# An RWKV-7 and mixture kernel: TensorE's order written out in passes 1 to 4, x placed one piece later, raw transfers and stores moved on SyncE's queue

## The chip, the cores and the metric

The kernel runs on one core of a Trainium2 chip. The metric is the device time of one execution in microseconds (us), lower is better. Engines are called as in the profile: PE is TensorE's matmuls, PEld its weight loads, DVE is VectorE, ACT is ScalarE, POOL is GpSimd, and SP is SyncE, which here only issues transfers.

## The reference

Two blocks follow each other. The first is a recurrence over 768 tokens for 4 batches and 8 heads of width 40, the second a mixture of four experts over the 3072 rows that come out of it.

```python
for t in range(S):                      # S = 768, state is (4, 8, 40, 40)
    y[:, :, t] = einsum('bhd,bhde->bhe', rt, state)
    Sa = einsum('bhde,bhe->bhd', state, at)
    state = state * wt[:, :, None, :] - einsum('bhd,bhe->bhde', Sa, bt) + einsum('bhd,bhe->bhde', vt, kt)
x = y.transpose(0, 2, 1, 3).reshape(3072, 320)
p = domain_probs / (domain_probs.sum(-1, keepdims=True) + 1e-09)
for e in range(4):                      # w1[e] is 320 x 1024, w2[e] is 1024 x 320
    out += p[:, e:e+1] * (np.maximum(x @ w1[e], 0) @ w2[e])
```

All numbers are float32.

## The kernel before

The 768 tokens are cut into 12 chunks of 64. A *unit* is one chunk of two batches, so there are 24 units; units 2c and 2c+1 make chunk c.

What a unit needs without the state is in the generator `within`, cut into steps by `yield`. For units 3 and later: (W1) `G`, the running product of the decays, from `rawW` by a transpose on DVE; (W2) `pg` on PE, `gp` and its reciprocal on DVE (L418, L419); (W3) `N` and `K` (L455, L459), `AT` (L228, L463) and the transposes of `rawV` and `rawR` into `VT` and `RT` (L228), all on DVE; (W4) `pNT` and `pKT` on PE (L340) with copies on ACT (L441); (W5) `pc` from `VT` and `RT` (L376) and the masked copy into `VC` on DVE (L387); (W6) `pfe` (L376) and the copy of `F` on ACT (L489); (W7) the masked copy `ET` on DVE (L387); (W8) `pev` on PE.

`substitute` solves a triangular system for all heads of a unit: a few instructions on DVE (`blocks`, `M`, L528 to L550) and then a chain of small operations on `Z`, on GpSimd for units 2 and later (L555 to L572). `merge` turns the result (`Qc`, `QTc`, L583 and L585), copies it with GpSimd (`QT`, L591), and joins it on PE by `pY` and `pQ` (L599), with copies of `Yq` on ACT between the two (L606).

What needs the state is in `step`: (S1) `prn`, `RH` on DVE; (S2) `psat`, `SaT` on ACT; (S3) `pxr`, the masked copy `SX` on DVE; (S4) `pdy`, `Y` and the new state on DVE (L694 to L705); (S5) x, the transposed input of the mixture: for the first two chunks by 12 matmuls into `pxT` (L711) and a copy (L715), later by 12 transfers on SyncE (L723).

The mixture is cut into *pieces* that wait in the list `todo`. For units 0 and 1 it is done unit by unit (`mixture_of_unit`): an *up* (w1 with Relu, `ph` and `hs`, L738, L752, L757) comes in pairs, a *down* (w2, `po`, L796) follows, and its product is added to `osb` on DVE (L771, L773); the last down of a unit also stores its rows (L778). From chunk 1 on a piece works on both units of a chunk (`mixture_of_chunk`): wide ups, sums of `hs` on DVE (`a`, L867), and products `down_1` and `down_2` (L873). Weights come in `w1p` or `sums` (L287), each load begun when the piece that used its buffer is done.

Pass u of the main loop runs the rest of W for unit u+1, S3 to S5 of unit u, W of unit u+2, the substitution of unit u+2, the merge of unit u+1 and S1, S2 of unit u+1. At four places, `gap(0)` to `gap(3)`, it takes pieces from `todo`. Passes 1 to 4 are *early* (`EARLY = 5`, so `u < EARLY`; pass 0 stands ahead of the loop); they take one piece a gap, and two at gaps 2 and 3 of pass 4.

The order in which instructions stand in the program is not the order in which they run. A scheduler simulates the program and gives each engine, at each moment, the earliest instruction that is ready in its simulation; the orders that come out are fixed for the run. `keep_in_program_order` ties an instruction behind the one that was written before it on the same engine; it adds no wait. In the kernel before, the early units' instructions on DVE, the substitution and the weight loads are tied so; of the matmuls only a few are.

`load_raw` makes transfers of the raw inputs; those of V and R of unit u+3, 16 of them, go into the list `later`, from which `begin_later` takes six after each piece (three where a gap takes two), and, in every pass, what is left, ahead of the second piece:

```python
        begin_later(len(later))
        run(w, 1)
        if not early:
            run(m, 1)
        gap(1)
```

Of the kernel before, what the change touches and what calls it, by code (L numbers as in the profile page):

```python
# [15 lines left out]
def kernel(  # L16
# [38 lines left out]
    nc = tc.nc  # L55
# [3 lines left out]
    P = 128  # L59
# [4 lines left out]
    NF = F // P  # L64
    NU = NC * B // 2
    DT = DM - 2 * P

    const = ctx.enter_context(tc.tile_pool(name="const", bufs=1))
    sb = ctx.enter_context(tc.tile_pool(name="sb", bufs=1))
# [98 lines left out]
    EARLY = 5  # L168
# [137 lines left out]
    def normalize():  # L306
        n = B // 2 * NC
        pp = big("pp")
        flat = probs.rearrange("p i t e -> p (i t) e")
        for e in range(E):  # L310
            nc.tensor.transpose(out=pp[:, e * n:(e + 1) * n], in_=flat[:, :, e], identity=ident[0:n, 0:n])
# [24 lines left out]
    def turn(name, src, pinned=False):  # L336

        p = big(name)
        for j in range(NJ):
            ins = nc.tensor.transpose(out=p[:, j * P:(j + 1) * P], in_=src(j), identity=ident[:])  # L340
            if pinned and j == 0:
                tc.keep_in_program_order(ins)
        return p
# [26 lines left out]
    def quadrants(p, lo, order, out_cols, *terms):  # L370


        for j, s, i in order:
            for n, term in enumerate(terms):
                row, col, at, lhsT, rhs = term(j, s, i)
                nc.tensor.matmul(  # L376
                    out=p[row][half(col), lo + at * out_cols:lo + (at + 1) * out_cols], lhsT=lhsT, rhs=rhs,
                    start=(n == 0), stop=(n == len(terms) - 1),
                )
        return [by(x[:, lo:lo + NJ * out_cols], out_cols) for x in p]  # L380
# [197 lines left out]
    def merge(q):  # L578


        Qc = sb.tile([P, H, Q], FP32, name="Qc", tag="q", bufs=2)
        QTc = sb.tile([P, H, Q], FP32, name="QTc", tag="q", bufs=2)
        tc.keep_in_program_order(nc.vector.transpose(out=dealt(Qc[:]), in_=q.Z))  # L583
        tc.keep_in_program_order(
            nc.vector.transpose(  # L585
                out=QTc[:].rearrange("p h r -> p (h r)"), in_=Qc[:].rearrange("p h c -> p (h c)"),
            )
        )
        q.QT = QTs()
        for i in range(P // Q):  # L590
            ins = nc.gpsimd.tensor_copy(out=q.QT[quarter(i), :, quarter(i % 2)], in_=QTc[quarter(i)])  # L591
            tc.keep_in_program_order(ins)
        yield

        def two_heads(name, lhsT, rhs, to):
            p = big(name)
            for n in range(NJ):
                for r in range(2):
                    nc.tensor.matmul(  # L599
                        out=p[half(r), n * 2 * Q:(n + 1) * 2 * Q], lhsT=lhsT[half(r), 2 * n:2 * n + 2, :],  # L600
                        rhs=rhs[half(r), 2 * n:2 * n + 2, :], start=True, stop=True,
                    )
# [12 lines left out]
    def step(q, xT):  # L615
# [92 lines left out]
        if placed:  # L708
            px = big("pxT")
            for n, (g, j) in enumerate(PLACES):  # L710
                nc.tensor.matmul(  # L711
                    out=px[:, g * P:(g + 1) * P], lhsT=pick[:, n, :], rhs=Y[:, j].rearrange("p i t -> p (i t)"),
                    start=(n == 0 or PLACES[n - 1][0] != g), stop=(n + 1 == len(PLACES) or PLACES[n + 1][0] != g),
                )
            nc.scalar.copy(out=xT, in_=px[:, 0:3 * P].rearrange("p (g t) -> p g t", g=3))  # L715
# [14 lines left out]
    def up_last(k, xT, n):  # L730

        w1 = pieces[k]
        ph = [ps.tile([P, HF // 2, n], FP32, name="ph", tag="mm", bufs=3) for _ in range(2)]

        for f in range(HF // 2):
            for c in range(2):
                for i in range(2):
                    nc.tensor.matmul(  # L738
                        out=ph[i][half(c), f, :], lhsT=w1.last[part(i), f, half(c)],
                        rhs=xT[part(i), 2, :], start=(f == 0), stop=False,  # L740
                    )
        return ph

    def up_main(k, xT, n, ph):

        w1 = pieces[k]
        h = sb.tile([P, HF, 2 * P], FP32, name="hs", tag="hs", bufs=3)
        for i in range(2):
            for f in range(HF // 2):
                for g in range(2):  # L750
                    at = i * HF // 2 + f
                    nc.tensor.matmul(  # L752
                        out=ph[i][:, f, :], lhsT=w1.main[:, g, at * P:(at + 1) * P],
                        rhs=xT[:, g, :], start=False, stop=(g == 1 and f == HF // 2 - 1),
                    )
# [27 lines left out]
    def mixture_of_unit(q):  # L783

        hs, at = {}, 2 * E * q.u

        def ups(e):
            hs[e] = [up(at + 2 * e + x, q.xT, P) for x in range(2)]
            used(at + 2 * e + 2)
            if q.u == 0 and e + 2 < E:  # L790
                load_w2(e + 2)

        def down(e):
            po = ps.tile([P, DM], FP32, name="po", tag="mm", bufs=3)
            for f in range(NF):
                nc.tensor.matmul(  # L796
                    out=po[:], lhsT=hs[e][f // HF][:, f % HF, 0:P], rhs=w2_sb[e][:, f, :],
                    start=(f == 0), stop=(f == NF - 1),
                )
            if e == 0:  # L800
                q.osb = outputs()
            add(q.osb[:], po[:], scale(q, e), e == 0)
            if e == E - 1:
                store(q, q.osb)

        todo.append(lambda: ups(0))
        for e in range(E):
            todo.append(lambda e=e: down(e))
            if e + 1 < E:
                todo.append(lambda e=e: ups(e + 1))  # L810
# [25 lines left out]
    def mixture_of_chunk(qs, xT):  # L836
# [32 lines left out]
        def products(name, *terms):  # L869
            p = ps.tile([P, len(terms) * HD], FP32, name=name, tag="mm", bufs=3)  # L870
            for n, (a, b) in enumerate(terms):
                for f in range(HF):
                    nc.tensor.matmul(  # L873
                        out=p[:, n * HD:(n + 1) * HD], lhsT=a[:, f, :], rhs=b[:, f, :],
                        start=(f == 0), stop=(f == HF - 1),
                    )
            return p
# [52 lines left out]
        last[:] = before  # L930


    todo, last, later = [], [], []

    def begin_later(n):
        for move in later[:n]:
# [3 lines left out]
    def mix(n):  # L940

        for piece in todo[:n]:
            piece()
            begin_later(3 if n > 1 else 6)
        del todo[:n]

# [22 lines left out]
    def keep_warm(n):  # L969

        for _ in range(n):
            ins = nc.tensor.matmul(out=warm[:, 0:P], lhsT=ident[:], rhs=ident[:], start=True, stop=True)
            tc.keep_in_program_order(ins)

    ws = [within(units[u]) for u in range(3)]
# [79 lines left out]
    sums_at.update({4 * 4 + 3: 2, 4 * 5 + 0: 3, 4 * 5 + 1: 2, 4 * 5 + 2: 3})  # L1055
    sum_ops = (None for e in range(E) for _ in add_weights(e))
    for u in range(1, NU):
        q = units[u]
        m = s_next = w = w_next = iter(())
        if u + 1 < NU:  # L1060
# [8 lines left out]
            mix((1 if at in sparse else 2) if pieces is None else pieces)  # L1069

        early = u < EARLY
        run(w_next, 99 if early else 1)
        run(s, 1)
        gap(0)
# [16 lines left out]
        gap(1)  # L1091

        if u + 3 < NU:
            go(load_raw(begin(u + 3), "WA"))
# [39 lines left out]
        s = s_next  # L1134
# [31 lines left out]
```

## Time and profile before

| | before |
|---|---|
| three timed runs | 1135.22, 1136.07, 1136.14 us (median 1136.07) |
| profiled execution | 1129.6 us, span of the instructions 1127.5 us |
| mean granted clock of TensorE | 0.986 |
| TensorE idle from 94.1 to 243.9 us (passes 1 to 4) | 14.2 of 149.8 us |
| TensorE idle from 287 to 1127 us | 9.8 of 840 us |

The span is that of one profiled execution. A stretch's idle time is its length less the busy time of TensorE in it, from the busy times by stretches. The names of tiles in the profile have no unit numbers: units are told apart by the order of their appearance. Names are written out<-in, and a line such as L376 or L752 is that of the helper that records the matmul, so blocks are told apart by the tile they write. A transfer's row on SyncE is the time of its issue, not of the data.

### The profile page before, as it was taken

The page shows a single profiled execution, that of the slowest core. Times are in us where ns is not written, and L with a number is a line of the kernel's source. Part 1 is how long each engine was busy: PE and PEld are TensorE (multiplying, and loading weights), DVE is VectorE, ACT ScalarE, POOL GpSimd, SP SyncE. Part 2 cuts the span into 40 slices and gives each one's busy share as a digit, 9 for nine tenths or more (in the row PEclk, how much of TensorE's full clock was granted, in tenths as well). Part 3 has the DMA queues.
Part 4 walks back from the last instruction along what each step waited for, and adds up shares of the span by engine and source line. Part 5 has one row for each costly group of instructions (what it writes and reads, how often), then busy time and mean ns, then how long its engine had stood idle before and what let it go on. Part 6 is the DMA issues. An engine that isn't in the chain of part 4 may idle for free.

```text
span 1127.5 us, 38551 instructions
## 1 busy us (share of the span) xinstructions
PE 1083.1 (96%) x16100; PEld 963.2 (85%) x16100; DVE 758.8 (67%) x1553; ACT 353.0 (31%) x956; POOL 498.8 (44%) x1272
## 2 busy tenths in 40 slices
PE   6899997999999999999999999999999999999998
PEld 5777776788989889988989989989899999888887
DVE  8766547797766767677677677677677686553343
ACT  2323423332332332432432332332333323321110
POOL 5005727754625526437437347346346356340000
PEclk7899998999999999999999999999999999999999
DMA  7784553245253543644543543544553442231320
GB/s 118 214 239 125 130 113 71 71 108 126 77 130 88 122 102 99 141 103 93 143 104 88 143 103 90 142 96 96 133 114 86 122 110 63 76 90 57 108 90 12
DMA packets 268868, 122.18 MB, mean 108 GB/s; under 512 B 213736, under 2 KB 242072, under 8 KB 268696
## 3 DMA queue, kind: packets, MB, share of 16 engines
q1 hardware_dynamic: 265416, 119.12, 43.4%
q8 instruction: 127, 2.08, 0.8%
q10 hardware_dynamic: 3280, 0.61, 0.3%
q14 instruction: 45, 0.37, 0.1%
HBM read 111.79 MB, written 3.93 MB: 103 GB/s over the span
## 4 chain that ended last, share of the span: by engine, by line
PE 67%; POOL 10%; DVE 7%; issue 4%; ACT 2%; SPq 1%; DMA 1%; DVEq 0%; POOLq 0%
PE p L873 23%; PE ph L752 22%; PE ph L738 7%; POOL Z L572 6%; POOL Z L559 4%; PE pdy L376 2%; PE psat L376 2%; PE po L796 2%; DVE M L534 1%; PE pxr L376 1%; PE prn L376 1%; PE pQ L599 1%; PE pfe L376 1%; DVE G L406 1%; PE pc L376 1%
## 5 line engine op out<-in xcount | busy, mean ns | idle before, releaser
L752 PE MATMUL ph<-xT,w1p 128*128 128x256 f32 (+1 forms) x1520 | 342.7, 378 | 1.7 <-issue 1.7
L752 PEld LDWEIGHTS ph<-xT,w1p 128*128 128x128 f32 x1520 | 273.4, 190 | 63.1 <-issue 25.6
L572 POOL TENSOR_TENSOR Z<-Z 128x31 f32<-128x31 f32 (+7 forms) x704 | 257.2, 365 | 55.2
L867 DVE TENSOR_TENSOR a<-hs 128x512 f32<-128x512 f32 x220 | 153.8, 716 | 104.6 <-ACT hs L757 104.6
L559 POOL TENSOR_TENSOR Z<-M,Z 128x62 f32<-128x62 f32 (+7 forms) x352 | 144.0, 409 | 134.5 <-DVE M L550 108.7
L757 ACT ACTIVATE hs<-ph 128x512 f32<-128x512 f32 (+1 forms) x208 | 115.3, 564 | 235.3 <-PE ph L752 234.3
L873 PE MATMUL p<-sums,a 128*128 128x160 f32 x1056 | 165.1, 299 | 0.0
L873 PEld LDWEIGHTS p<-sums,a 128*128 128x128 f32 x1056 | 152.9, 190 | 2.3
L773 DVE SCALAR_TENSOR_TENSOR osb<-p,gate,osb 128x320 f32<-128x320 f32 (+1 forms) x243 | 107.9, 482 | 55.3 <-PE p L873 52.1
L531 POOL COPY below<-F 32x256 f32<-32x256 f32 x48 | 23.4, 488 | 219.5 <-ACT F L489 217.8
L738 PE MATMUL ph<-xT,w1p 64*64 64x256 f32 (+1 forms) x1520 | 111.1, 379 | 5.4 <-issue 5.4
L873 PE MATMUL p<-w,a 128*128 128x160 f32 x704 | 105.8, 301 | 0.9 <-ACT hs L757 0.5
L873 PE MATMUL p<-w,hs 128*128 128x160 f32 x704 | 102.9, 299 | 0.0
L873 PEld LDWEIGHTS p<-w,hs 128*128 128x128 f32 x704 | 100.3, 190 | 2.2
L873 PEld LDWEIGHTS p<-w,a 128*128 128x128 f32 x704 | 98.3, 190 | 3.6 <-ACT hs L757 3.6
L591 POOL COPY QT<-QTc 32x256 f32<-32x256 f32 x96 | 49.3, 513 | 91.4 <-DVE QTc L585 44.9
L738 PEld LDWEIGHTS ph<-xT,w1p 64*64 64x64 f32 x1520 | 66.1, 135 | 14.3 <-issue 9.8
L534 DVE STREAM_TRANSPOSE M<-blocks 128x1024 f32<-128x1024 f32 x24 | 47.2, 1968 | 33.9 <-ACT blocks L528 33.7
L679 ACT COPY RS<-pxr 64x256 f32<-64x256 f32 x88 | 32.2, 366 | 115.0 <-DVE SX L387 73.6
L419 DVE RECIPROCAL gp<-gp 128x320 f32<-128x320 f32 x24 | 51.7, 2153 | 0.8
L516 ACT COPY EV<-pev 64x160 f32<-64x160 f32 x96 | 23.4, 286 | 88.1 <-PE pev L376 87.7
L583 DVE STREAM_TRANSPOSE Qc<-Z 128x256 f32<-128x256 f32 x24 | 15.1, 631 | 49.1 <-POOL Z L572 48.9
(151 smaller groups left out, 1427.9 us busy)
## 6 DMA issues: line engine op xcount, KB each, us to landing
w1p<-in_moe_w_dram SPq DMA_DIRECT2D x95, 512.0 KB
w1p<-in_moe_w_dram SPq DMA_DIRECT2D x190, 64.0 KB
w<-in_moe_w_dram SPq DMA_DIRECT2D x4, 1280.0 KB
sums<-in_moe_w_dram SPq DMA_DIRECT2D x9, 512.0 KB
natW<-in_w_dram SPq DMA_DIRECT2D x48, 80.0 KB
natB<-in_b_dram SPq DMA_DIRECT2D x48, 80.0 KB
natK<-in_k_dram SPq DMA_DIRECT2D x48, 80.0 KB
out_dram<-osb SPq DMA_DIRECT2D x46, 80.0 KB
```

The lines of the kernel that those rows point to most:

```text
L376: nc.tensor.matmul(out=p[row][half(col), lo + at * out_cols:lo + (at + 1) * out_cols], lhsT=lhsT, rhs=rhs, start=(n == 0), stop=(n == len( ...
L419: pin(nc.vector.reciprocal(out=gp[:], in_=gp[:]))
L534: ins = nc.vector.transpose(out=M[:], in_=cols)
L559: ins = eng.tensor_tensor(out=Z[:, 1:3, 0:n, j + 1:Q], in0=M[:, j:j + 2, None, j + 1:Q].to_broadcast([P, 2, n, m]), in1=Z[:, here, 0:n, j: ...
L572: eng.tensor_tensor(out=z[:, 0], in0=z[:, 0], in1=z[:, x], op=ALU.add)
L591: ins = nc.gpsimd.tensor_copy(out=q.QT[quarter(i), :, quarter(i % 2)], in_=QTc[quarter(i)])
L738: nc.tensor.matmul(out=ph[i][half(c), f, :], lhsT=w1.last[part(i), f, half(c)], rhs=xT[part(i), 2, :], start=(f == 0), stop=False,)
L752: nc.tensor.matmul(out=ph[i][:, f, :], lhsT=w1.main[:, g, at * P:(at + 1) * P], rhs=xT[:, g, :], start=False, stop=(g == 1 and f == HF // ...
L757: nc.scalar.activation(out=h[:, i * HF // 2:(i + 1) * HF // 2, 0:n], in_=ph[i][:], func=ACTF.Relu,)
L773: nc.vector.scalar_tensor_tensor(out=to, in0=p, scalar=sc, in1=to, op0=ALU.mult, op1=ALU.add)
L867: nc.vector.tensor_tensor(out=t[:], in0=x, in1=y, op=op)
L873: nc.tensor.matmul(out=p[:, n * HD:(n + 1) * HD], lhsT=a[:, f, :], rhs=b[:, f, :], start=(f == 0), stop=(f == HF - 1),)
```

## The change

Four things, all for passes 1 to 4 of the loop, except that the store of the two units is moved wherever its piece stands.

1. All matmuls and transposes on TensorE go through two helpers that tie each behind the one written before it, while `in_order[0]` is set.
2. S5, which places x, runs after the piece of gap 1, no longer ahead of W3 and that piece. The mixture of the unit or chunk joins `todo` after it.
3. What is left in `later` is begun at the head of the pass, ahead of the piece of gap 0, no longer after it.
4. The store of a unit's rows (units 0 and 1) is begun after the next piece, no longer with the last down.

```diff
+    in_order = [False]
+
+    def stated(ins):
+        if in_order[0]:
+            tc.keep_in_program_order(ins)
+        return ins
+
+    def matmul(**k):
+        return stated(nc.tensor.matmul(**k))
...
-            ins = nc.tensor.transpose(out=p[:, j * P:(j + 1) * P], in_=src(j), identity=ident[:])
+            ins = transpose(out=p[:, j * P:(j + 1) * P], in_=src(j), identity=ident[:])
...
             if e == E - 1:
-                store(q, q.osb)
+                stores.append(lambda: store(q, q.osb))
...
         for piece in todo[:n]:
+            ready = stores[:]
+            del stores[:]
             piece()
+            for begin_store in ready:
+                begin_store()
             begin_later(3 if n > 1 else 6)
...
     for u in range(1, NU):
+        in_order[0] = u < EARLY
         q = units[u]
...
         early = u < EARLY
+        if early:
+            begin_later(len(later))
         run(w_next, 99 if early else 1)
         run(s, 1)
         gap(0)
...
         run(w, 1)
         if not early:
             run(w_next)
-        run(s)
+            run(s)
+
+        if early:
+            run(w, 1)
+            gap(1)
+            run(s)
         if u == 1:
             mixture_of_unit(q)
         elif q.bp:
             mixture_of_chunk(units[u - 1:u + 1], chunks_x[q.c])
-        begin_later(len(later))
-        run(w, 1)
         if not early:
+            begin_later(len(later))
+            run(w, 1)
             run(m, 1)
-        gap(1)
+            gap(1)
```

All other calls of `nc.tensor.matmul` and `nc.tensor.transpose` are replaced in the same way.

More of the change, by code (lines that the diff above doesn't have):

```diff
@@ L66, with transpose @@
     DT = DM - 2 * P
+    in_order = [False]
[5 more added lines that the diff above has]
+        return stated(nc.tensor.matmul(**k))
+    def transpose(**k):
+        return stated(nc.tensor.transpose(**k))
     const = ctx.enter_context(tc.tile_pool(name="const", bufs=1))
@@ L310, in normalize @@
         for e in range(E):
-            nc.tensor.transpose(out=pp[:, e * n:(e + 1) * n], in_=flat[:, :, e], identity=ident[0:n, 0:n])
+            transpose(out=pp[:, e * n:(e + 1) * n], in_=flat[:, :, e], identity=ident[0:n, 0:n])
         nc.scalar.copy(out=gate[:], in_=pp[:, 0:E * n].rearrange("p (e b c) -> p c b e", b=B // 2, c=NC))
@@ L375, in quadrants @@
                 row, col, at, lhsT, rhs = term(j, s, i)
-                nc.tensor.matmul(
+                matmul(
                     out=p[row][half(col), lo + at * out_cols:lo + (at + 1) * out_cols], lhsT=lhsT, rhs=rhs,
@@ L598, in two_heads @@
                 for r in range(2):
-                    nc.tensor.matmul(
+                    matmul(
                         out=p[half(r), n * 2 * Q:(n + 1) * 2 * Q], lhsT=lhsT[half(r), 2 * n:2 * n + 2, :],
@@ L710, in step @@
             for n, (g, j) in enumerate(PLACES):
-                nc.tensor.matmul(
+                matmul(
                     out=px[:, g * P:(g + 1) * P], lhsT=pick[:, n, :], rhs=Y[:, j].rearrange("p i t -> p (i t)"),
@@ L737, in up_last @@
                 for i in range(2):
-                    nc.tensor.matmul(
+                    matmul(
                         out=ph[i][half(c), f, :], lhsT=w1.last[part(i), f, half(c)],
@@ L751, in up_main @@
                     at = i * HF // 2 + f
-                    nc.tensor.matmul(
+                    matmul(
                         out=ph[i][:, f, :], lhsT=w1.main[:, g, at * P:(at + 1) * P],
@@ L795, in down @@
             for f in range(NF):
-                nc.tensor.matmul(
+                matmul(
                     out=po[:], lhsT=hs[e][f // HF][:, f % HF, 0:P], rhs=w2_sb[e][:, f, :],
@@ L872, in products @@
                 for f in range(HF):
-                    nc.tensor.matmul(
+                    matmul(
                         out=p[:, n * HD:(n + 1) * HD], lhsT=a[:, f, :], rhs=b[:, f, :],
@@ L930, in mixture_of_chunk @@
         last[:] = before
-    todo, last, later = [], [], []
+    todo, last, later, stores = [], [], [], []
     def begin_later(n):
@@ L971, in keep_warm @@
         for _ in range(n):
-            ins = nc.tensor.matmul(out=warm[:, 0:P], lhsT=ident[:], rhs=ident[:], start=True, stop=True)
+            ins = matmul(out=warm[:, 0:P], lhsT=ident[:], rhs=ident[:], start=True, stop=True)
             tc.keep_in_program_order(ins)
```

## The prediction

> **What bounds the kernel now.** I read the page first, then the busy time by stretches, then the instructions of VectorE and GpSimd in order of time, then the waits of TensorE and of SyncE's queue between 86 and 250 us. The page's busy times and its row of granted clock:
>
> ```profile
> PE 1083.1 (96%) x16100; PEld 963.2 (85%) x16100; DVE 758.8 (67%) x1553; ACT 353.0 (31%) x956; POOL 498.8 (44%) x1272
> ...
> PEclk7899998999999999999999999999999999999999
> ```
>
> TensorE is the bound, and its clock is short of full at the start and once more in the seventh slice. The changed passes are where that is. By first appearances of `pev` and `psat`, pass 1 starts at about 94.1 us, pass 2 at 127.5, pass 3 at 171.7, pass 4 at 202.7, and what is stated for pass 4 is done at 243.9. Busy us by stretch (PE, weight loads, DVE, ACT, POOL), then granted clock, DMA share, GB/s:
>
> ```profile
> 94.10:243.90 149.80, 135.64 (x2361) 112.33 (x2360) 100.89 (x196) 52.86 (x153) 90.17 (x230) 0.97 0.45 103
> 150.50:161.10 10.60, 10.60 (x86) 8.01 (x84) 1.87 (x3) 2.88 (x7) 0.00 (x0) 1.00 0.52 96
> 177.20:180.60 3.40, 1.18 (x11) 1.15 (x11) 3.40 (x9) 0.00 (x0) 2.93 (x7) 1.00 0.00 0
> 180.60:184.10 3.50, 3.50 (x25) 2.81 (x27) 3.30 (x6) 1.65 (x3) 3.03 (x7) 0.51 0.19 44
> 190.00:194.30 4.30, 0.91 (x49) 0.94 (x53) 2.10 (x5) 1.61 (x5) 2.46 (x10) 1.00 0.73 119
> 194.30:197.70 3.40, 3.40 (x78) 2.94 (x70) 3.37 (x5) 1.86 (x8) 2.30 (x5) 0.50 0.81 223
> 207.90:211.40 3.50, 3.50 (x66) 3.10 (x68) 3.36 (x4) 1.26 (x4) 2.95 (x8) 0.51 0.04 7
> 287.00:1127.00 840.00, 830.18 (x12075) 749.96 (x12074) 556.55 (x1131) 254.41 (x674) 366.30 (x932) 1.00 0.41 101
> ```
>
> Two regimes: from 287 us on, TensorE idles 1.2%; in the four passes it idles 149.80 - 135.64 = 14.2 us (9%), and three stretches of 3.4 us run at half clock. GpSimd does nothing from 150.5 to 161.1, yet at 190 to 194.3 TensorE waits for its result. Why, shows on VectorE and GpSimd (in brackets the idle time before the instruction, and what ended it):
>
> ```profile
> 145.12 0.70 DVE L228 STREAM_TRANSPOSE VT<-rawV 128x512 f32<-128x512 f32 x1
> 154.99 0.55 DVE L773 SCALAR_TENSOR_TENSOR osb<-po,gate,osb 128x320 f32<-128x320 f32 x1 [9.17 <-PE po L796]
> 155.46 0.70 DVE L228 STREAM_TRANSPOSE RT<-rawR 128x512 f32<-128x512 f32 x1
> 156.08 0.78 DVE L833 TENSOR_TENSOR sums<-w 128x640 f32<-128x640 f32 x1
> 161.89 0.78 DVE L387 COPY_PREDICATED VC<-mask_up,pc 128x256 f32<-128x256 int32 x2 [5.02 <-PE pc L376]
> ```
>
> ```profile
> 144.47 0.51 POOL L572 TENSOR_TENSOR Z<-Z 128x8 f32<-128x8 f32 x2
> 164.08 1.73 POOL L591 COPY QT<-QTc 32x256 f32<-32x256 f32 x4 [19.10 <-DVE ET L387]
> ```
>
> The last `rawR` transfer of unit 4 was issued at 140.79, so RT could have been turned soon after 145. It stands behind an `osb` addition whose product `po` TensorE had pulled ahead. RT holds back `pc` and `pfe` of unit 4 (161.1 instead of some 146), these hold back the substitution on GpSimd (169.2 to 192.1, idle 19.1 us before), and `pY` waits for that at 193.4. So the early passes are bound by the unit chain, through an order. The waits of TensorE and SyncE there:
>
> ```profile
> PE pY L599 <- DVE QTc L585: 5.8, 4, 3.4
> PE pxT L711 <- DVE Y L699: 2.2, 1, 2.2
> ```
>
> ```profile
> SPq L778 <- DVE osb L773: 25.8, 2, 17.5
> ```
>
> [...]
>
> **The change, part by part.**
>
> *Work in the four passes.* Blocks from the PE timeline. A unit's share: pev 0.6, pxr 1.0, pdy 1.8, pg 0.5, pxT 1.4, pNT and pKT 0.9, pc 0.5, pfe 1.0, pY 0.5, prn 1.1, pQ 0.6, psat 1.1, together 11.0 us. A pair of narrow ups takes 5.1 (145.42 to 150.48), a down 4.4 (150.48 to 154.88), a wide up 4.75, down_1 3.3, down_2 4.35. Passes 1 to 3 have 19.0 us of pieces each (two pairs and two downs; in pass 3 two wide ups replace a pair and a down), pass 4 has 3 x 4.75 + 2 x 3.3 + 4.35 = 25.2 without pxT. Sum: 3 x 30.0 + 34.8 = 124.8. The passes take 149.8, so 25.0 us are overhead: 14.2 idle, up to 3 x 3.41 / 2 = 5.1 lost to the clock, the remaining 5.7 in blocks stretched by latency (pdy from 173.4 to 176.5).
>
> *TensorE in stated order.* No instruction is added; only the order changes. In passes 2 and 3 it puts pc and pfe of unit u+2 ahead of ups and downs now pulled before them. Unit 4's pfe then ends near 148 and its substitution, 23 us long, near 176, while pY of unit 4 is due near 185: the 3.4 us wait goes, and the two half-clock stretches in pass 3 with it. What order costs, pass by pass, since nothing can step in:
> - Pass 1: pev waits for ET (96.7) from 94.2, where an up now fills part: 2.6. pc waits for RT: after pdy, VectorE needs 5.8 us to K (103.9 to 109.7), then AT, its product, VT and RT, 2.75, against pg, down, pxT, pNT and pKT, 7.2: 1.3. pQ waits for four Yq copies behind F and blocks on ACT: 1.0. Together 4.9.
> - Pass 2: pxr for SaT 0.3, pc 0.8, pQ 0.7, and the unexplained 1.66 at 131.5 kept: 3.5.
> - Pass 3: 0.3 + 0.5 + 0.7 = 1.5.
> - Pass 4: down_1 is shorter and no pxT covers N and K: 2.1. pc 1.4, pxr 0.3, pQ 0.7, SX behind the sums of h (five of 0.72) 1.5: 6.0.
>
> Sum 15.9. Of the 5.7 in stretched blocks I keep half, 2.9 (ends 0 and 5.7). New overhead 18.8, gain 25.0 - 18.8 = 6.2 us. Ends: all stretch kept, two half-clock stretches (3.4) and 3 more behind VectorE in pass 4: 28.0, a loss of 3; half of the waits: 8 + 1.5, a gain of 15.5.
>
> *x behind the second gap's piece.* pxT (12 matmuls, 1.34) and its copy (0.48) move behind a down of 4.4; Y is ready by then, so the 2.2 us wait at 177.3 goes (counted above). Its reader, the up of gap 2, comes after pNT, pKT and pc, 1.4 us later, and covers the copy. In pass 4, x is 12 transfers on SyncE, 9.05 us of issue (219.79 to 228.84); they move behind a weight load (3 issues) and stay ahead of the next unit's loads; their reader is in pass 5. Cost 0, bounds -0.5 to +0.5.
>
> *Raw transfers at the head.* At most four rawR issues (139.22 to 141.23, 2.0 us) go before the weight load of gap 0 instead of after it; that load comes 2.0 us later, with some 20 us until its pair. Value 0 by itself: no VectorE wait for a transfer appears between 86 and 250. Bounds -1 to +0.5.
>
> *Stores later.* Two stores of two issues (1.15 us) move behind 16 loads of the next unit and a weight load. SyncE's waits of 8.3 and 17.5 us go; queued behind them were rawW, rawA, natW, natB, natK, natV, and nobody waits for those in 86 to 250. Two osb buffers, next asked for a pass later. Value 0, bounds -1 to +0.5.
>
> After 244 us TensorE does the same work and is busy 98.8%, so what is gained early stays. The sum stands against the profiled span of 1127.5: 1121.3. The three timed runs are at 1135.22 to 1136.14; as a difference of work it carries over: 1136.1 - 6.2 = 1129.9.
>
> **The rivals.**
> - *The gain is given back* (within 0.2%). The waits moved to VectorE could be as long as those removed: in passes 2 to 4 it is busy 78.3 of 116.4 us, and 32.3 of the last 41.2. Shorter passes raise that; each pc, N and K later is a TensorE stop that nothing fills. Total overhead 23 to 27: 1134 to 1138. Against it: RT, the worst, is freed by construction.
> - *Slower: pass 4 stalls in order.* The place is pNT of unit 6 behind gp, N, K and ten sums of h on VectorE, then pc behind RT. At 5 us for each of the two instead of 2.1 and 1.4 that is 6.5 more, with two half-clock stretches 3.4, and pass 1's half-clock stretch 1.7: 18.8 + 11.6 = 30.4, 5.4 us slower, 1141.5. It decides once the overhead of the four passes is over 27.3. For it: in pass 4 TensorE now escapes such waits by reordering, with 2.9 us idle. Against it: the wide up before each of them is 4.75 us of cover.
> - *The change doesn't do what it says.* An order edge binds only TensorE; if VectorE's queue still has RT behind a later addition, TensorE would have to stop for it. It can't be the addition of down 2, which now comes after pc; a raw transfer still late would cost 2 to 4 us, 1132 to 1134.
>
> **How the numbers follow.** A measurement of this kernel can tell 0.2%, 2.3 us, from no change. The forecast (gain over 2.3) has 0.75, two thirds of it between 1124 and 1132; the case that gives back, and the late transfer where it leaves no more, 0.14; slower 0.11. The range 1122.5 to 1137.5 leaves out a tenth on either side: gains of over 13.5 and losses of over 1.5 us.
>
> **What would show it.** Right: pc and pfe of unit 4 before its second pair of ups; the GpSimd pause of 19.1 us down to a few; substitution of unit 4 done before 180; no half-clock stretch in pass 3; the mark now at 243.9 near 237.7; everything after it shifted alike. Steps wrong: pev or pNT waits over 3 us, half clock after them, or the VectorE row at 9 in the slices of pass 4. The prediction is wrong if the mark does not move, or if it moves and the steady passes give it back by waits for weights.

## The result and the profile after

The changed kernel takes 1123.51 us (median of six executions, 1122.3 to 1127.3), the kernel before beside it 1136.11 (six, 1131.57 to 1138.23). The ratio is 0.9898, 95% interval 0.9873 to 0.9923, so it is faster by 1.0%. The changed kernel's profiled execution took 1122.36, with a span of 1120.2 us.

All lines of the changed kernel stand 13 further down from the first helper on. All its matmuls are recorded at L76 and its transposes at L79, so blocks must be told by their tiles. First the page: busy times and granted clock.

```profile
PE 1076.8 (96%) x16100; PEld 961.0 (86%) x16100; DVE 757.0 (68%) x1553; ACT 353.2 (32%) x956; POOL 501.9 (45%) x1272
...
PEclk8899999999999999999999999999999999999999
```

With the same 16100 matmuls TensorE is busy for 6.3 us less (1083.1 before): work at half clock counts as busy (3.40 of 3.40 us from 270.5, below), and so does a block that runs stretched: `pdy` of pass 3 before stands from 173.37 to 176.44 at full clock, with TensorE busy for 2.25 of the 2.30 us from 174.1; the same 64 matmuls take 1.81 in pass 2 (136.57 to 138.38). Next the busy times by stretch (length; PE, weight loads, DVE, ACT, POOL; clock, DMA share, GB/s): passes 1 to 4 from the first `pev` of pass 1 to the mark (the end of the last stated piece of pass 4), the three half-clock stretches, the rest.

```profile
94.90:232.80 137.90, 126.90 (x2361) 107.66 (x2360) 100.94 (x197) 52.61 (x153) 98.90 (x245) 0.99 0.52 119
209.10:212.50 3.40, 2.99 (x100) 2.90 (x104) 3.29 (x8) 0.15 (x2) 1.63 (x5) 0.50 0.09 22
270.50:273.90 3.40, 3.40 (x69) 3.05 (x64) 2.70 (x7) 1.63 (x6) 0.00 (x0) 0.50 0.91 227
318.20:321.60 3.40, 3.40 (x78) 2.97 (x78) 2.89 (x7) 0.00 (x0) 0.00 (x0) 0.51 0.81 218
287.00:1120.00 833.00, 822.89 (x11930) 743.41 (x11928) 551.55 (x1120) 252.06 (x668) 360.60 (x911) 1.00 0.41 101
```

The four passes hold the same 2361 matmuls and take 137.9 us in place of 149.8. One half-clock stretch is left in them, and two stand in passes 5 and 6, where the kernel before had none. What such a stretch costs is put at half its length, 1.7 us. This is an estimate: behind the 32 matmuls of the first half of `pfe` the second half starts after 0.46 us at clock 1.00 (147.64 to 148.10) and after 0.86 us at clock 0.50 (210.39 to 211.25). The rows of VectorE and of GpSimd that showed the cause before now read:

```profile
144.49 0.45 DVE L786 SCALAR_TENSOR_TENSOR osb<-po,gate,osb 128x320 f32<-128x320 f32 x1
144.85 0.52 DVE L468 SCALAR_TENSOR_TENSOR n_tok<-natB,gp 128x320 f32<-128x320 f32 x1
145.30 0.55 DVE L472 TENSOR_TENSOR k_tok<-natK,gp 128x320 f32<-128x320 f32 x1
145.77 0.70 DVE L241 STREAM_TRANSPOSE VT<-rawV 128x512 f32<-128x512 f32 x1
146.40 0.67 DVE L241 STREAM_TRANSPOSE RT<-rawR 128x512 f32<-128x512 f32 x1
146.99 0.78 DVE L846 TENSOR_TENSOR sums<-w 128x640 f32<-128x640 f32 x1
147.89 0.79 DVE L400 COPY_PREDICATED VC<-mask_up,pc 128x256 f32<-128x256 int32 x2
```

```profile
150.08 1.74 POOL L604 COPY QT<-QTc 32x256 f32<-32x256 f32 x4 [1.93 <-DVE ET L400]
```

RT of unit 4 follows VT at once, and `VC`, which reads `pc`, comes 1.5 us after RT instead of 6.4. GpSimd pauses 1.93 us, no longer 19.1. On TensorE `pc` now waits for RT, and the ups come after it:

```profile
147.12 0.69 PE L76 MATMUL pc<-RT,VT 40*64 40x64 f32 x32 [0.50 <-DVE RT L241]
...
148.57 4.62 PE L76 MATMUL ph<-xT,sums 64*64 64x128 f32 x59
```

What is left of TensorE's and of SyncE's waits between 86 and 250 us, the largest of each (in total, times, longest):

```profile
PE pc L76 <- DVE RT L241: 2.9, 3, 1.5
PE pev L76 <- DVE ET L400: 2.6, 1, 2.6
PE pNT L79 <- DVE n_tok L468: 2.3, 1, 2.3
PE pQ L76 <- ACT Yq L619: 1.3, 1, 1.3
```

```profile
SPq L300 <- PE ph L76: 15.8, 8, 6.6
SPq L736 <- DVE state L717: 10.8, 2, 8.4
```

`pY` and `pxT` are no longer among the waits, nor is the store of `osb` with its 25.8 us.

### The profile page after: what moved, and what is told of

Its sections match the earlier page's. It is cut to its first block, busy times and chain, and to the rows that moved or that the text cites. A ratio compares the mean times of both kernels' runs of the same rounds, so it can differ in the third digit from the quotient of the medians.

```text
span 1120.2 us, 38531 instructions
## 1 busy us (share of the span) xinstructions
PE 1076.8 (96%) x16100; PEld 961.0 (86%) x16100; DVE 757.0 (68%) x1553; ACT 353.2 (32%) x956; POOL 501.9 (45%) x1272
## 4 chain that ended last, share of the span: by engine, by line
PE 59%; POOL 12%; DVE 9%; issue 5%; ACT 4%; SPq 2%; DMA 2%; DVEq 0%; POOLq 0%
PE ph L76 26%; PE p L76 20%; POOL Z L585 8%; POOL Z L572 4%; PE psat L76 2%; PE pdy L76 2%; DVE M L547 1%; SPq L223 1%; PE pxr L76 1%; PE po L76 1%; PE pfe L76 1%; PE pQ L76 1%; DVE G L419 1%; ACT Yq L619 1%; PE prn L76 1%
## 5 line engine op out<-in xcount | busy, mean ns | idle before, releaser
L76 PE MATMUL ph<-xT,w1p 128*128 128x256 f32 (+3 forms) x3040 | 446.0, 378 | 7.8 <-issue 7.8
L76 PEld LDWEIGHTS ph<-xT,w1p 64*64 64x64 f32 (+1 forms) x3040 | 338.3, 162 | 76.6 <-issue 33.8
L76 PE MATMUL p<-sums,a 128*128 128x160 f32 x1056 | 164.8, 299 | 0.0
L76 PEld LDWEIGHTS p<-sums,a 128*128 128x128 f32 x1056 | 152.9, 190 | 2.2
L76 PE MATMUL p<-w,a 128*128 128x160 f32 x704 | 106.2, 301 | 1.3 <-ACT hs L770 0.8
L76 PE MATMUL p<-w,hs 128*128 128x160 f32 x704 | 102.9, 299 | 0.0
L76 PEld LDWEIGHTS p<-w,a 128*128 128x128 f32 x704 | 98.3, 190 | 4.4 <-ACT hs L770 4.4
L76 PEld LDWEIGHTS p<-w,hs 128*128 128x128 f32 x704 | 100.2, 190 | 2.2
L604 POOL COPY QT<-QTc 32x256 f32<-32x256 f32 x96 | 50.3, 524 | 75.2 <-DVE QTc L598 35.1
L596 DVE STREAM_TRANSPOSE Qc<-Z 128x256 f32<-128x256 f32 x24 | 15.0, 627 | 46.4 <-POOL Z L585 46.3
L619 ACT COPY QT<-pQ 32x128 f32<-32x128 f32 x96 | 24.7, 257 | 58.9 <-PE pQ L76 57.2
L651 ACT COPY SN<-prn 128x256 f32<-128x256 f32 x44 | 15.0, 371 | 80.4 <-DVE RH L646 77.6
```

Of the source, the lines that this page charges most:

```text
L76: return stated(nc.tensor.matmul(**k))
```

## The experiments

The executions of one kernel spread over 3 to 13 us, and the first `pc` of pass 1 stands between 88.0 us (order in passes 2, 3) and 94.3 us (order alone) in these profiles. So two lengths inside one profile are compared, besides the ratio: from the first `pc` of pass 1 to the mark, and from the mark to the end of the last matmul of the mixture. Pass lengths run from one end of `psat` to the next; what is pulled ahead over such an end counts for the earlier pass. Ratios are to the kernel before, run beside each kernel. In us:

| kernel | ratio [95%] | pc to mark | mark to end | passes 1, 2, 3, 4 |
|---|---|---|---|---|
| before | 1 | 155.4 | 879.1 | 46.9, 44.2, 31.0, 37.8 |
| before, again | | 153.9 | 880.9 | 46.7, 42.6, 31.1, 37.8 |
| changed | 0.9898 [0.9873, 0.9923] | 143.6 | 883.3 | 48.7, 31.7, 30.5, 37.1 |
| changed, again | 0.9900 [0.9862, 0.9938] | 143.4 | 879.5 | 48.6, 31.7, 30.5, 36.9 |
| order alone | 0.9927 [0.9900, 0.9955] | 150.4 | 878.6 | 50.2, 34.9, 33.1, 36.5 |
| changed, no order | 0.9978 [0.9963, 0.9992] | 150.6 | 880.6 | 46.6, 38.2, 35.3, 34.9 |
| tie on VectorE | 1.0010 [0.9997, 1.0024] | 155.9 | 883.6 | 46.7, 46.4, 31.8, 35.3 |
| changed, x as before | 0.9947 [0.9927, 0.9967] | 147.7 | 881.3 | 50.1, 33.6, 32.3, 36.1 |
| changed, raw and stores as before | 0.9899 [0.9866, 0.9933] | 143.5 | 879.3 | 48.7, 31.9, 31.5, 35.8 |
| order in passes 2, 3 | 0.9832 [0.9795, 0.9868] | 138.0 | 880.2 | 46.6, 31.7, 30.5, 33.5 |
| order in pass 2 | 0.9833 [0.9802, 0.9864] | 138.1 | 883.4 | 46.7, 31.7, 30.6, 33.4 |
| changed, rawW first | 0.9832 [0.9794, 0.9870] | 146.4 | 873.9 | 50.0, 31.6, 30.5, 38.7 |
| before, rawW first | 0.9933 [0.9909, 0.9957] | 154.8 | 876.4 | 46.7, 43.5, 31.1, 37.8 |
| order in 2, 3, rawW first | 0.9803 [0.9773, 0.9833] | 138.2 | 875.8 | 46.9, 31.7, 30.5, 33.4 |

**Order alone.** The kernel before with the two helpers and, at the head of the loop,

```diff
+        in_order[0] = u < EARLY
```

while x, raw transfers and stores stay as before.

> The kernel before with the stated TensorE order in passes 1 to 4 alone; x, raw transfers and stores as before. If the order on TensorE is the cause (theory), pc and pfe of unit 4 come at about 147 to 149 us, the mark (243.9 before, 232.9 after) stands at 232 to 236 and the time is within 3 us of the changed kernel's. pxT now stands ahead of a down with nothing to cover Y: three waits of 1.5 to 2 us for Y more than in the changed kernel. If the raw transfers or the stores are the cause (rival), TensorE stops in order for RT, and the time is within 4 us of the kernel before.

Measured: ratio 0.9927, pc to mark 150.4, of which one more half-clock stretch in pass 1 (103.4 to 106.8, clock 0.51) takes some 1.7 by the estimate above; the pass is 1.5 longer than in the changed kernel. `pc` of unit 4 comes 62.7 us after the first `pc`, where it was 72.6 before and is 57.9 in the changed kernel. Passes 2 and 3 together take 68.0 us; they took 75.2 before (73.7 in its second profile) and take 62.2 in the changed kernel. So order alone makes about half of the gain of these two passes: TensorE now stands before `pxT` for 1.16 and 1.10 us, and the passes take 3.2 and 2.6 us more than in the changed kernel. The time is as near to the changed kernel's as expected. `pc` of unit 4 (157.0) and the mark (244.7) come later than expected, 5.1 us of it because the first `pc` comes at 94.3 and not at 89.2.

**Everything but the order.** In the changed kernel:

```diff
-        in_order[0] = u < EARLY
+        in_order[0] = False
```

What remains of the change are the later x, the raw transfers and the stores.

> The changed kernel with the stated order left out; x later, raw transfers at the head, stores later. If TensorE's order is the cause, at most a third of the gain is left (0 to 4 us against before). If earlier raw transfers are enough for the scheduler to see RT in time (rival), most of the gain stays: 6 to 12 us. By its compiled order one down no longer stands ahead of pc of unit 4 but two pairs of ups and a down are still there, so I expect 2 to 5 us and pc of unit 4 at about 155.

Measured: 0.9978, from pc to mark 4.8 us less than in the first profile of the kernel before and 3.3 less than in the second, 2.5 us (0.22%) in the times. `pc` of unit 4 comes 67.4 us after the first: RT stands behind the `osb` addition as before (156.36), and TensorE has ups, a down and ups ahead of `pc`. It waits 4.0 us for `QTc` and 3.6 for `QT`, and a half-clock stretch of 6.8 us begins in pass 3. Passes 2 and 3 together take 73.5 us. So order alone brings these two passes down by 7.2 us, the three moves without it by 1.7, all together by 13.0: part of the gain needs both.

**The tie on VectorE.** In the kernel before, the `osb` addition is tied behind the last turn of a raw input on VectorE (an order edge, no wait); TensorE stays free.

```diff
+            ins = add(q.osb[:], po[:], scale(q, e), e == 0)
+            if last_turn[0] is not None:
+                tc.add_manual_dep(
+                    ins.ins, last_turn[0].ins.name,
```

> The kernel before, with one order tie on VectorE: a unit's osb addition goes behind the last turn of RT written before it. Nothing on TensorE is tied. If VectorE's queue is what holds RT back and that alone is the cause (rival), RT of unit 4 is turned near 146, and the gain is 6 to 10 us. If it is TensorE's own order (theory), RT is turned near 146 and pc still stands behind the pulled-ahead ups: pc at 155 to 160, gain 0 to 3 us.

The instructions of VectorE around RT of unit 4 in this kernel:

```profile
145.55 0.71 DVE L228 STREAM_TRANSPOSE RT<-rawR 128x512 f32<-128x512 f32 x1 [0.75 <-DMA rawR<-in_r_dram]
146.19 0.78 DVE L840 TENSOR_TENSOR sums<-w 128x640 f32<-128x640 f32 x1
146.89 0.54 DVE L774 SCALAR_TENSOR_TENSOR osb<-po,gate,osb 128x320 f32<-128x320 f32 x1
155.34 0.55 DVE L774 SCALAR_TENSOR_TENSOR osb<-po,gate,osb 128x320 f32<-128x320 f32 x1 [7.91 <-PE po L797]
164.00 0.78 DVE L387 COPY_PREDICATED VC<-mask_up,pc 128x256 f32<-128x256 int32 x2 [8.12 <-PE pc L376]
```

RT is done at 146.3, as early as in the changed kernel, and `pc` still comes at 163.2. TensorE works meanwhile, with three waits of some 0.5 us between the last ups:

```profile
148.94 2.05 PE L754 MATMUL ph<-xT,sums 128*128 128x128 f32 x16
150.82 4.47 PE L797 MATMUL po<-w,hs 128*128 128x320 f32 x16
155.23 0.65 PE L740 MATMUL ph<-xT,w1p 64*64 64x128 f32 x8
...
163.22 0.69 PE L376 MATMUL pc<-RT,VT 40*64 40x64 f32 x32
```

The addition in front of RT was a symptom. What held unit 4 is TensorE's own order, which has `pc` behind a pair of ups, a down and a pair of ups. Why the scheduler's simulation placed it there is not shown. Time and stretch are those of the kernel before.

**x in its old place**, the rest of the change kept. In the changed kernel:

```diff
-            run(s)
-
-        if early:
-            run(w, 1)
-            gap(1)
-            run(s)
+        run(s)
...
-            run(w, 1)
+        run(w, 1)
+        if not early:
...
-            gap(1)
+        gap(1)
```

> The changed kernel with x placed where it was, ahead of the second gap's piece; stated order, raw transfers and stores as changed. The prediction put the move's worth at the wait of pxT for Y: in stated order pxT would wait about 1.6 us (Y, 0.75 + 0.7, after pdy) in each of passes 1 to 3, 3 to 5 us in all, against 0 if pg and the start of the down cover it (rival). The mark then stands at 236 to 238 instead of 232.9.

Measured: 147.7 from pc to mark, 4.1 more than the changed kernel. Passes 2 and 3 are 1.9 and 1.8 us longer, and `pxT` waits 1.29 and 1.13 us for `Y` in them. The half-clock stretch adds little to the difference: it lies in pass 1 here (1.4 us longer) and in pass 4 in the changed kernel (1.0 us longer there).

**Raw transfers and stores in their old places**, order and x kept.

```diff
-                stores.append(lambda: store(q, q.osb))
+                store(q, q.osb)
...
-        if early:
-            begin_later(len(later))
...
+            begin_later(len(later))
```

> The changed kernel, with the raw transfers and the unit stores where they were in the kernel before; TensorE's order and the place of x stay as changed. Theory of the prediction: both moves are worth nothing here (bounds -1 to +0.5 each), so first pc to mark is within 1.5 us of the changed kernel's, some 143 to 145, and the time within 2 us. Rival, that the late raw transfers hold back RT or VT now that the passes are shorter: SyncE waits 8 and 17 us for osb with raw transfers behind, pc of some unit waits for a transfer, and the stretch is 3 us or more longer.

Measured: 143.5 against 143.4 in the changed kernel run beside it, and the medians are 1122.09 and 1122.61. SyncE waits for `osb` again (11.3 us between 86 and 330), and no wait of TensorE in the four passes is over 0.4 us longer than in the changed kernel, but for one of 0.75 in front of `pxr`. With order and x in place, the times show no worth in the two moves. The profile hides up to 1.7 us by the estimate above: the changed kernel has a half-clock stretch in pass 4 (36.9 us in the run beside it) and this run has none in the four passes (35.8).

**The changed kernel again**, as a control.

> The changed kernel once more, beside the kernel before and the three kernels that follow, so that they can be held against it under the same conditions. Theory: the stretch from the first pc to the mark (the end of the last stated piece of pass 4) is again near 143.6 us, some 11 to 12 less than the 155.4 of the kernel before, and from the mark to the end it takes some 883, about 4 more than the 879.1 of before, with TensorE stopped twice inside ph of passes 5 and 6; the ratio is near 0.990. Rival, that the stops in passes 5 and 6 belong to one execution only: they are missing here, and the end comes some 4 us earlier, a ratio near 0.987.

Measured: pc to mark 143.4 (143.6 in the first profile), but mark to end 879.5 (883.3). The same program differs by 3.8 us after the mark. The stops in `ph` are there in both, here 1.98, 3.23 and 1.27 us, together 6.5 instead of 7.8, with one half-clock stretch instead of two (mean clock from the mark to 330 us 0.98, 0.96 in the first profile). The first expectation holds for the place of the stops, not for the size of what follows the mark.

**Order in passes 2 and 3 only.**

```diff
-        in_order[0] = u < EARLY
+        in_order[0] = u in (2, 3)
```

> The changed kernel, with TensorE's order stated in passes 2 and 3 only. The prediction gave the order in passes 1 and 4 nothing but costs (4.9 and 6.0 us of waits that nothing fills). Theory of the prediction: without it pass 1 fills the wait of pev and that of pc, pass 4 the one of pNT, and the first pc to the mark takes 1 to 4 us less than in the changed kernel, some 140 to 142.6. Rival, that order in these passes also keeps urgent matmuls ahead of pieces: the stretch gets longer by 1 to 4 us, because pc or pfe of unit 3 or 6 slips behind a piece again and its substitution starts later.

Measured: 138.0, which is 5.4 less than the changed kernel and more than the 1 to 4 us expected, and 8.7 us off the median of the changed kernel beside it (1113.92). Of the 8.7 the profiles thus show 5.4; the rest is not explained. Busy times by pass, first of the kernel before, then of the changed one, then of this:

```profile
80.60:127.50 46.90, 44.22 (x787) 36.39 (x782) 26.45 (x53) 17.91 (x53) 24.07 (x68) 1.00 0.54 118
127.50:171.70 44.20, 40.72 (x709) 33.04 (x700) 22.66 (x46) 16.18 (x48) 19.56 (x50) 1.00 0.51 120
171.70:202.70 31.00, 25.32 (x494) 20.16 (x494) 23.34 (x44) 11.66 (x32) 22.78 (x56) 0.89 0.35 72
202.70:240.50 37.80, 34.85 (x581) 29.94 (x573) 29.16 (x54) 13.32 (x38) 22.14 (x56) 0.95 0.35 76
```

```profile
81.40:130.10 48.70, 42.60 (x780) 35.47 (x775) 26.82 (x55) 17.85 (x52) 24.16 (x68) 1.00 0.61 138
130.10:161.80 31.70, 30.64 (x618) 25.70 (x610) 24.20 (x46) 13.35 (x40) 23.79 (x59) 1.00 0.46 88
161.80:192.30 30.50, 29.94 (x596) 25.09 (x588) 22.58 (x44) 14.06 (x40) 20.93 (x53) 1.00 0.50 116
192.30:229.40 37.10, 33.19 (x585) 28.55 (x577) 31.25 (x59) 13.47 (x37) 28.55 (x63) 0.95 0.46 104
```

```profile
80.20:126.80 46.60, 43.94 (x777) 36.22 (x771) 26.25 (x52) 17.78 (x52) 23.86 (x68) 1.00 0.63 144
189.00:222.50 33.50, 32.51 (x582) 27.40 (x574) 28.07 (x56) 13.57 (x37) 24.68 (x58) 1.00 0.44 96
```

By these ends the change gains 12.5 us in pass 2 and next to nothing in 3 and 4, and loses 1.8 in pass 1. But passes 2 and 3 have to be read together: the kernel before has 709 and 494 matmuls in them, the changed one 618 and 596, because ups and downs that were pulled ahead stood in pass 2. The idle time was largest in pass 3 (5.7 us, where `pY` and `pxT` waited). Over both, the time falls from 75.2 to 62.2 us and TensorE's idle time from 9.2 to 1.6, and two half-clock stretches go.

Stated order costs 2.1 us in pass 1 (48.7 against 46.6) and 3.6 in pass 4 (37.1 against 33.5): there the scheduler's own order fills the waits of `pev` (0.9 left of 2.6), `pNT` (0.5 of 2.3) and the first `pc`, and the half-clock stretch of pass 4 goes with them (clock 1.00 instead of 0.95).

**Order in pass 2 only.**

```diff
-        in_order[0] = u < EARLY
+        in_order[0] = u == 2
```

> The changed kernel with TensorE's order stated in pass 2 only. Theory, that the loss of the kernel before comes from one chain (RT of unit 4 behind the osb addition of a down pulled ahead, hence pc, pfe and substitution of unit 4 late, hence pY late): pass 2 again takes some 31.7 us between the ends of psat (44.2 before the change), first pc to mark is 138 to 140, and the time is within 2 us of the order in passes 2 and 3. Rival, that each pass has to be protected by itself: pc of unit 5 slips behind a piece of pass 3, which then takes 33 to 38 us instead of 30.5, and the stretch is 3 to 8 us longer than with the order in passes 2 and 3.

Measured: 138.1, passes 46.7, 31.7, 30.6, 33.4; ratio 0.9833. Pass 3 needs no order of its own: with unit 4 in time, the scheduler's order for it is as good. Everything but the order, above, differs from this kernel in one line alone, the order of pass 2: 150.6 against 138.1 from pc to mark, 0.9978 against 0.9833. With the moves in place, one chain caused the loss that order removes.

**rawW first.** In the changed kernel, for the passes from 5 on:

```diff
+        elif u + 3 < NU:
+            go(load_raw(begin(u + 3), "W"))
...
-            go(load_raw(begin(u + 3), "WA"))
+            go(load_raw(begin(u + 3), "WA") if early else load_raw(units[u + 3], "A"))
```

Why: in the changed kernel TensorE stops inside `ph` at 266.5 and 314.1. VectorE, TensorE and SyncE there (pass 5; `xT` are the twelve transfers of x):

```profile
264.11 0.93 DVE L241 STREAM_TRANSPOSE G<-rawW 128x256 f32<-128x256 f32 x2 [5.37 <-DMA rawW<-in_w_dram]
...
269.01 0.37 DVE L786 SCALAR_TENSOR_TENSOR osb<-p,minus_gate,osb 128x160 f32<-128x160 f32 x1
```

```profile
269.49 0.87 PE L76 MATMUL ph<-xT,w1p 64*64 64x256 f32 x11 [3.01 <-issue]
```

```profile
249.18 9.80 SPq L736 DMA_DIRECT2D xT<-Y  x12
259.08 1.65 SPq L300 DMA_DIRECT2D w1p<-in_moe_w_dram  x3
260.77 1.56 SPq L223 DMA_DIRECT2D rawW<-in_w_dram  x3
```

SyncE issues rawW behind 11.5 us of other issues; VectorE stands at its transpose for 5.37 us with `a` and the `osb` additions behind it; `ph` goes on 0.1 us after one of these additions is done. The profile calls TensorE's wait "issue", so that it waited for the addition is an inference.

> The changed kernel, with the transfers of rawW of unit u+3 begun at the head of each pass from 5 on, ahead of the 12 transfers of x and of the load of w1p on SyncE's queue; rawA stays where it was. Theory: the changed kernel loses some 4 us again in passes 5 and 6, because VectorE stands 5.4 and 8.0 us at the transpose of rawW with the sums a and the osb additions behind it. Here these two waits go, TensorE does not stop inside ph for 3.0 and 4.1 us, the two half-clock stretches after it go, and the mark to the end takes about 875 to 880 instead of 883: 4 to 9 us faster than the changed kernel, 1114 to 1120. Rival, that the stops have another cause (the profile calls them issue) or that x or w1p, now later, takes the place of rawW: no gain, 883 from the mark to the end, the stops at the same place or a new wait of ph for xT.

Measured: mark to end 873.9 against 879.5 (and 883.3), median 1113.21 against 1122.61, each a little lower than was expected. Of the 9.4 us of the medians the profiles show 5.6 after the mark. In this kernel:

```profile
242.17 1.86 SPq L223 DMA_DIRECT2D rawW<-in_w_dram  x4
...
254.47 8.90 SPq L736 DMA_DIRECT2D xT<-Y  x12
```

```profile
259.13 0.91 DVE L241 STREAM_TRANSPOSE G<-rawW 128x256 f32<-128x256 f32 x2
```

No wait stands before `G`, TensorE's stops in `ph` fall from 6.5 and 7.8 us to 0.9 (mark to 430), and no half-clock stretch follows the mark (clock 1.00). The longer pc to mark, 146.4, goes with two more half-clock stretches, one of 3.4 us in pass 1 and 3.4 us more in pass 4 (mean clock 0.97 from pc to mark, 0.99 in the changed kernel).

**rawW first in the kernel before.**

```diff
+        if not early and u + 3 < NU:
+            go(load_raw(begin(u + 3), "W"))
...
-            go(load_raw(begin(u + 3), "WA"))
+            go(load_raw(begin(u + 3), "WA") if early else load_raw(units[u + 3], "A"))
```

> The kernel before, with the transfers of rawW of unit u+3 begun at the head of each pass from 5 on, and nothing else changed. It tells whether the stops behind rawW came with the change or were there already. Theory, that the earlier passes made them: the kernel before stops only 1.7 us in passes 5 and 6, so its mark to end falls from 879.1 to some 877 and the time by 1 to 3 us. Rival, that rawW costs the kernel before as much as the changed one: mark to end 874 and the time 5 or more us lower, a ratio of 0.995 or less; then nothing was given back by the change, and the two kernels carry the same loss.

Measured: 876.4 from mark to end, 2.7 less than the first profile of the kernel before and 4.5 less than the second; the first theory has 877. But the ratio is 0.9933, 7.6 us, as the rival has it, and as large as what the edit gives the changed kernel (0.9832 against 0.9900). So the stops were not made by the change. Nor were they invisible: the waits of VectorE and of TensorE in the first profile of the kernel before, between 244 and 430 us, hold these two. Three of TensorE's four stops are those at 322.6, 366.8 and 412.2 us (1.18, 2.31 and 1.38); the last follows a wait of VectorE for rawA (4.23 us from 405.2).

```profile
DVE G L228 <- DMA rawW<-in_w_dram: 11.8, 2, 6.9
```

```profile
PE ph L738 <- issue: 5.4, 4, 2.3
```

Why the times gain 3 to 5 us more than the profiles show is not settled.

**The kernel before again**, for a second profile.

> The kernel before once more, for a second profile of it: the timed executions of it lie 3 to 6 us above the one that was profiled (1129.6), while those of the changed kernel lie about its own profile. Theory, that the first profile caught an execution with short stops behind rawW: first pc to mark is again 155 to 156, and the mark to the end takes 881 to 885 instead of 879.1, with stops inside ph of passes 6 to 8 of more than the 4.9 us of the first profile. Rival, that the difference lies in the start or is no more than scatter: mark to end within 1.5 us of 879.1.

Measured: 153.9 and 880.9, with stops in `ph` of 1.53, 2.40 and 1.06 us at 323.1, 367.7 and 413.2. That is 1.8 over the first profile, of the size of the scatter, and under the 881 of the theory. With 879.1 and 880.9 before and 883.3 and 879.5 after, a loss behind the mark is not shown.

**Both together.** The edit of rawW first, and in the same kernel

```diff
-        in_order[0] = u < EARLY
+        in_order[0] = u in (2, 3)
```

> Both improvements on the changed kernel together: TensorE's order stated in passes 2 and 3 only, and the transfers of rawW begun at the head of the passes from 5 on. Theory, that the two act in different stretches and add: first pc to mark 138 us as with the order in passes 2 and 3 (143.4 in the changed kernel), mark to end about 875 (879.5 in the changed kernel, 873.9 with rawW first), together some 10 us under the changed kernel, 1105 to 1111. Rival, that both only removed one and the same slack, so that the gain of the second is lost elsewhere (in waits for weights in passes 5 and 6, which now come earlier still): no more than the better of the two alone, 1112 to 1114.

Measured: 138.2 and 875.8, 8.9 us under the control in the profile, where the two alone gained 5.4 before the mark and 5.6 behind it. So each acts in its own stretch, but they do not add in full. The median is 1111.35, just above the range of the theory; the ratio 0.9803 is the lowest of all, though its interval overlaps those of the two parts. In the times it is 1.0% below the changed kernel (0.9900), where each alone is 0.7% below. Stops of this kind remain: VectorE stands 5.25 us from 384.7 for rawA, whose transfers were not moved, and TensorE stops in `ph` for 2.53 us at 391.5. The kernel beats the one before and the changed one, by 2.0% and about 1.0%.

## Why the prediction was right, and where its sizes were off

**The mechanism held.** `pc` of unit 4 starts at 147.1 and `pfe` ends at 148.8 (near 148 was said); the substitution of unit 4 ends at 177.5 (before 180); GpSimd's pause is 1.9 us; pass 3 has no half clock. The tie on VectorE and the order in pass 2 show that it was TensorE's order, in this one chain. The prediction's wording, RT holds back `pc`, took the visible wait for the link that had to be freed. Its own lines speak against it: RT is done at 156.2, and `pc` starts at 161.1, behind more ups. The lead it gave (TensorE had pulled `po` ahead) was the right one.

**The gain was under-sized.** The mark moved to 232.8, not 237.7. From the first `pev` to the mark the passes take 137.9; less the 124.8 of work, the new overhead is 13.1 us, not 18.8. Term by term:

- Waits: 11.0 instead of 15.9. Pass 1 has 5.5 (4.9 was said; `pev` 2.61, `pc` 1.48, `pQ` 1.33). Pass 2 has 1.1, not 3.5: the unexplained 1.66 of `ph` is gone, and so are `pQ`'s 0.7 here and in the later passes. The 1.66 is in part luck: the stop comes and goes by execution. The second profile of the kernel before has none, and its pass 2 is 1.6 us shorter; the kernel before with rawW first has 0.93. Pass 3 has 0.6, not 1.5. Pass 4 has 3.9, not 6.0: `pNT` 2.26 and `pc` 0.91 (2.1 and 1.4 were said), and nothing for SX behind the sums.
- Half clock: none was in the sum; one stretch is there (209.1, clock 0.50), 3.4 / 2 = 1.7 by the estimate above. Of the three stretches of before, the prediction gave a reason for the two in pass 3 to go. The one in pass 4 (207.9) it dropped without one, and one stands there still (209.1), now behind the wait of `pNT`.
- Stretched blocks: 2.9 was kept, 13.1 - 11.0 - 1.7 = 0.4 is left. It was halved for want of a reason, and in proportion it is the term that was mis-sized most; in us the waits are. That the stretch belonged almost wholly to the same stops is inferred from what is left, and the 124.8 is an estimate.

These make 4.9 - 1.7 + 2.5 = 5.7 us, and the prediction's 6.2 becomes 11.9. The median lies only 1.0 us above the low end of the stated range, and just under 1124 to 1132, where most of the forecast's chance was put.

**Moves.** x was given cost 0, with the 2.2 us wait counted in the order's gain. Undone alone it costs 1.9 and 1.8 us in passes 2 and 3, so of the 11.9 about 3.7 need the move: in stated order `pxT` would wait in both passes. Raw transfers and stores at 0 fits the times (undone, the median is 0.5 lower); the profile leaves up to 1.7. All three moves without the order gain 2.5 us in the times. What x alone, or the raw transfers and stores alone, do to the kernel before was not run.

**"What is gained early stays"** holds within the scatter: mark to end is 881.4 on average of two profiles after, 880.0 before. The 98.8% behind it, an average over 840 us, hid 5.4 us of stops in passes 5 to 8, of a kind that both kernels carry. The forecast of the time, 1129.9, was 6.4 above the first median; the passes account for 5.7 of that.

**The rivals.** Given back: refuted, with 13.1 us of overhead against the 23 it needs. Slower through pass 4: the place was right (order costs pass 4 3.6 us, `pNT` with a half-clock stretch after it), the price was not. That RT could stay behind a later addition did not happen.

## What to carry to other kernels

When an engine waits behind an instruction that came early, free the engine that ran ahead, not the queue where the wait shows; the cheapest test is an order edge on each of the two alone. State an order only where the scheduler's choice delays a chain, here one pass in four: in the first and the last the same edge removed fillers and cost 2.1 and 3.6 us. When the order has moved work over the end of a pass, read the two passes together. And look for short stops inside a stretch that averages 98.8% busy: moving four transfers ahead of twelve others took another 9.4 us off the median.

## What the runs showed of the hardware

Between 60 and 1080 us the profile of the kernel before has three stretches of 3.41 us at clock 0.50, and so has that of the changed kernel. In the 3.41 us ahead of each, TensorE was busy for 1.19, 0.90 and 1.73 us (before: stretches from 180.6, 194.3 and 207.9) and for 1.12, 1.02 and 0.14 us (changed: from 209.1, 270.5 and 318.3). The clock behind each is 1.00 again.

The 2.6 us wait of `pev` is not in every profile followed by half clock. In the changed kernel TensorE is busy for 1.93 us from 92.99 to 96.40 and for 2.24 us from 96.40 to 99.82, and the clock stays at 1.00. With order alone it is busy for 0.77 us in a stretch of the same length, and the next runs at half clock:

```profile
99.98:103.40 3.42, 0.77 (x32) 0.64 (x34) 3.27 (x9) 0.00 (x0) 0.86 (x4) 1.00 0.62 182
103.40:106.80 3.40, 3.40 (x71) 3.07 (x64) 2.57 (x7) 0.95 (x4) 2.93 (x7) 0.51 0.82 231
```

Of the six profiles with this wait of 2.6 us, three go on at full clock, and their pass 1 takes 48.6 to 48.7 us (changed, changed again, raw and stores as before). Three go on at half clock, and it takes 50.0 to 50.2 (order alone, x as before, rawW first). Of these three, rawW first has pass 1 written as in the changed kernel. So one and the same wait costs 1.3 to 1.6 us more in some profiles than in others; what decides it is not shown. That would fit the spread of the executions, but no run tests it.
